# Neighbour sums on one core: output scaling moved to ScalarE, self terms added by the transfer, buckets decoded by shift and xor

## The chip, the core and the metric

The kernel runs on one core of a Trainium2 chip. A core has a matrix engine (PE; PEld is its weight load), a vector engine (DVE), an activation engine (ACT), a general engine (POOL) and a queue for transfers (SP); POOL and ACT issue transfers too, and 16 DMA engines carry all of them. Each engine runs its own instructions in order, and waits only on semaphores. The metric is the time on the device in microseconds (us), as the median of repeated executions; the profile is of one further execution.

## The reference

One layer of a graph network with mean aggregation: for 800,000 edges, the feature rows of the source nodes are summed at the destination nodes, scaled by `deg_inv`, and passed through a small weight.

```python
N, deg, D = 12500, 64, 64            # nodes, edges per node, features; E = N * deg

def reference(x, src, dst, deg_inv, w_self, w_neigh):
    nsum = _segment_sum(x[src], dst, N)          # (N, 64), random src and dst
    h_neigh = nsum * deg_inv[:, None]
    return x @ w_self + h_neigh @ w_neigh
```

## The kernel before

The edges are sorted first, and then gather and scatter both become matrix products with one-hot matrices.

**Keys and sort.** Each edge becomes a 32-bit key (`make_keys`): destination block of 144 nodes, source block of 128 nodes, then a bit for the half of the destination block and the two offsets inside the blocks. A pair of blocks is a bucket; there are 87 x 98 = 8526. 128 partitions sort 6250 keys each on DVE (`sort_runs`, L223 with copies on ACT at L225), the runs are cut at bucket borders, gathered by POOL (`gather_runs`, L461) and merged on DVE (`merge_runs`, L272 and L284 with copies on ACT at L268). The buckets are handled in two parts: part 0 has 41 buckets a row on 128 rows, part 1 has 27. The merge of part 1 is cut into steps that are dealt out by a written order (`after_sort`, `sums_and_merge`, under a manual schedule) between the decode of part 0 and the first tiles of the loop over buckets.

**Decode.** For each bucket POOL gathers a window of keys (`gather_window`, L621, tile `v`). `decode_buckets` works on four windows at once: `split` on DVE takes the bucket's base off the keys by xor (L668), counts on DVE the keys that belong there, with the count in `cnt` (L670), shifts the source offset out (L672, tile `w`) and masks the destination offset (L673); `narrow` on ACT turns both into 16-bit numbers (L678, L682) and stores the source offsets to `sl`; `turn` transposes the destination offsets on PE into `dlT`. Keys that lie beyond a window are found by `beyond`, and handled as extra edges ("leftovers"). The counts are summed at the end (`check`); if they don't come to the number of edges, a slow general path runs.

**Loop over buckets.** `one_hots` reloads `sl` for 28 buckets at a time to all partitions (tile `slb`, on SP's queue, L785) and compares it on DVE: `ohs` (L787) and `ohd` (L790). `nodes` goes over tiles of 8 buckets. PE picks source rows: `ct` <- `xh`, `ohs` (L815, three buffers in PSUM); ACT copies `ct` to `xg` (L825), and from tile 540 on DVE copies some of them (L823); PE sums at the destinations: `acc` <- `ohd`, `xg` (L871). Seven destination blocks make an octet, 86 tiles. At its end come the leftovers: their source rows are fetched by POOL (tile `lx`, L852, with an index that DVE copies out first, L850), and DVE makes their one-hots (tile `ohl`, L864, two instructions for each chunk of 128 keys).

**Output.** `self_terms` computes `x @ w_self` during the sort and stores it to a scratch tensor `own` in blocks of 1024 rows, through two buffers `os`. After an octet, `finish` handles its two blocks of 504 nodes, in steps dealt out between tiles: load `own` (tile `fo`, L923, SP's queue), multiply by `w_neigh` on PE (L939), copy the result to `o` on ACT (L940, one instruction of 256 columns), scale by `deg` on DVE (L945), add `fo` on DVE (L946), store to `out` (L947, POOL's queue; SP's for the last block).

## Time and profile before

| what | value |
|---|---|
| median of 3 runs | 2080.38 us (2077.32 to 2090.19) |
| the profiled execution | 2089.12 us, its span 2087.4 us |
| DVE busy | 1937.5 us, 93% of the span |
| ACT busy | 1257.6 us, 60% |
| PE busy | 1023.8 us, 49% |
| POOL busy | 589.7 us, 28% |
| moved | 330.78 MB, 158 GB/s over the span |

How to read it: a row of a group gives the line, the engine, the operation, output and input tiles with their shapes and the count, then the busy time in us and the mean duration of one in ns, and behind the second bar the idle time of the engine just before, with what ended it. A row of the waits names who waited, for whom, the total in us, how many times, and the longest. A row of the timeline begins with the start and the duration in us. The share of busy time is a mean over stages with different limits; what matters for a change is the stage in which it lies. The profiled execution lies 8.7 us above the median.

### The profile page before, as it was taken

The numbers are of one execution on the slowest core, as the hardware profiler recorded it, in microseconds if no ns is written. First come the engines' busy times: TensorE is split into PE (matmuls) and PEld (weight loads), VectorE is DVE, ScalarE is ACT, GpSimd is POOL, SyncE is SP. The second block draws the span as 40 slices with busy tenths as digits, with TensorE's granted clock in tenths as the row PEclk, the third lists the DMA queues.
The fourth block names the chain that finished last, engine by engine and source line by source line (L and its number), as shares of the span: only waits on it lengthen the run. The fifth ranks groups of instructions, "written<-read, shape, count | busy, mean of one in ns | idle before, by whom it ended". The sixth has DMA issues, their size and how long they took to land.

```text
span 2087.4 us, 59594 instructions
## 1 busy us (share of the span) xinstructions
PE 1023.8 (49%) x26057; PEld 887.0 (42%) x26057; DVE 1937.5 (93%) x2144; ACT 1257.6 (60%) x1779; POOL 589.7 (28%) x867
## 2 busy tenths in 40 slices
PE   0060000000000000000799999999987889989897
PEld 0050000000000000000688788788776778878786
DVE  8999999998999999999999899999999988988887
ACT  7470000078100010532799999999988788888886
POOL 1000000007898889878401010010152001000000
PEclk9999999999999999999999999999999999999999
DMA  4150000010100000111777787777876677777774
GB/s 152 48 115 9 0 0 0 16 47 17 23 20 22 13 14 11 53 54 50 273 292 286 261 285 280 273 277 268 306 268 251 222 288 286 291 268 284 269 286 161
DMA packets 108220, 330.78 MB, mean 158 GB/s; under 512 B 53680, under 2 KB 61824, under 8 KB 107440
## 3 DMA queue, kind: packets, MB, share of 16 engines
q1 hardware_dynamic: 90784, 306.65, 40.0%
q0 software_dynamic: 14352, 18.65, 4.2%
q8 instruction: 205, 3.36, 0.6%
q10 hardware_dynamic: 2816, 1.61, 0.3%
q14 instruction: 63, 0.52, 0.1%
HBM read 307.86 MB, written 18.99 MB: 157 GB/s over the span
## 4 chain that ended last, share of the span: by engine, by line
PE 37%; DVE 28%; POOL 19%; issue 10%; ACT 5%; DMA 1%; DVEq 0%; ACTq 0%; POOLq 0%; SPq 0%
PE ct L815 21%; PE acc L871 14%; POOL u L461 13%; DVE b L223 9%; DVE a L223 8%; POOL pad L372 3%; ACT xg L825 2%; POOL v L621 2%; DVE ohd L790 2%; DVE ohs L787 2%; DVE u L284 1%; PE po L939 1%; DVE xg L823 1%; DVE junkd L444 1%; ACT junk L598 1%
## 5 line engine op out<-in xcount | busy, mean ns | idle before, releaser
L825 ACT ACTIVATE xg<-ct 128x1024 f16<-128x1024 f32 (+1 forms) x991 | 935.2, 1111 | 104.0 <-PE ct L815 84.1
L815 PE MATMUL ct<-xh,ohs 128*128 128x128 f16 x8526 | 604.7, 222 | 52.5 <-issue 22.8
L815 PEld LDWEIGHTS <-ohs 128*128 128x128 f16 x8526 | 500.1, 99 | 98.4 <-issue 42.7
L284 DVE TENSOR_TENSOR u<-u 128x256 f32<-128x256 f32 (+47 forms) x494 | 452.2, 946 | 22.6 <-ACT u L268 15.6
L461 POOL DMA_INDIRECT u<-d,ix x256 | 327.3, 1279 | 470.6 <-DVE junkd L444 429.3
L871 PE MATMUL acc<-ohd,xg 64*128 64x72 f16 x17052 | 410.0, 195 | 52.9 <-issue 30.3
L787 DVE TENSOR_SCALAR ohs<-slb,pidx 128x3584 f16<-128x3584 bf16 x305 | 350.1, 1148 | 32.2 <-PE ct L815 30.4
L871 PEld LDWEIGHTS <-xg 64*128 64x128 f16 x17052 | 324.1, 95 | 128.6 <-issue 47.9
L790 DVE TENSOR_TENSOR ohd<-iota,dlT 128x2016 f16<-128x2016 bf16 x305 | 365.9, 1200 | 0.0
L688 PE MATMUL tr<-idb,l 128*128 128x128 bf16 x68 | 9.3, 277 | 463.9 <-ACT l L682 460.5
L268 ACT ACTIVATE u<-u 128x256 f32<-128x256 f32 (+15 forms) x94 | 47.4, 594 | 282.4 <-DVE u L272 282.4
L223 DVE TENSOR_TENSOR b<-a 128x3120 f32<-128x3120 f32 (+38 forms) x106 | 205.8, 1993 | 3.2 <-ACT junka L442 0.5
L688 PEld LDWEIGHTS <-l 128*128 128x128 bf16 x68 | 5.7, 120 | 467.1 <-ACT l L682 463.8
L223 DVE TENSOR_TENSOR a<-b 128x3114 f32<-128x3114 f32 (+33 forms) x92 | 189.2, 2104 | 3.1 <-ACT b L225 2.0
L947 POOL DMA_DIRECT2D out<-o x24 | 22.8, 952 | 574.5 <-DVE o L946 491.7
L451 PE MATMUL stp<-idf,st 128*128 128x128 f32 x2 | 0.9, 448 | 360.0 <-DVE st L449 360.0
L451 PEld LDWEIGHTS stp<-idf,st 128*128 128x128 f32 x2 | 0.4, 182 | 360.5 <-issue 360.5
L225 ACT ACTIVATE a<-b 128x1 f32<-128x1 f32 (+44 forms) x57 | 22.2, 423 | 204.0 <-DVE b L223 201.4
L823 DVE CAST xg<-ct 128x1024 f16<-128x1024 f32 x78 | 95.2, 1221 | 49.6 <-PE ct L815 49.5
L852 POOL DMA_INDIRECT lx<-xt,lxi x28 | 48.2, 1720 | 301.3 <-PE ct L815 165.8
L621 POOL DMA_INDIRECT v<-d,ix x68 | 90.8, 1335 | 61.0 <-ACT ix L651 43.6
L372 POOL MEMSET pad<- 128x89 f32 x457 | 90.3, 198 | 9.4
(135 smaller groups left out, 821.5 us busy)
## 6 DMA issues: line engine op xcount, KB each, us to landing
slb<-sl SPq DMA_DIRECT2D x305, 896.0 KB
u<-d,ix POOLq DMA_INDIRECT x256, 2.5
xt<-xh SPq DMA_DIRECT2D x1, 3136.0 KB
own<-os SPq DMA_DIRECT2D x12, 256.0 KB
fo<-own SPq DMA_DIRECT2D x24, 126.0 KB
out<-o POOLq DMA_DIRECT2D x24, 126.0 KB, 4.5
rd<-dst SPq DMA_DIRECT2D x4, 521.0 KB
rs<-src SPq DMA_DIRECT2D x4, 521.0 KB
```

Source lines behind the costliest of these rows:

```text
L223: nc.vector.tensor_tensor(view(dst, lo + sh, [[st, g], [1, l]]), x, y, op=op)
L284: nc.vector.tensor_tensor(to, at(cur, ln + lo, n), at(cur, lo + k, n), op=op)
L372: self.nc.gpsimd.memset(self.pad, 0.0)
L461: nc.gpsimd.indirect_dma_start(out=u[:nr, p * w:(p + 1) * w], out_offset=None, in_=src, in_offset=bass.IndirectOffsetOnAxis(ap=self.start[ ...
L621: self.nc.gpsimd.indirect_dma_start(out=self.v[:, k].bitcast(F32), out_offset=None, in_=flat(self.d2[part], 128 * PITCH2[part]), in_offset ...
L787: nc.vector.tensor_scalar(s.rearrange("p c s -> p (c s)"), b, self.pidx[:, :1], None, op0=OP.is_equal)
L790: nc.vector.tensor_tensor(d, self.iota[:, None].to_broadcast([128, 14, HN, 2]), ix, op=OP.is_equal)
L815: nc.tensor.matmul(ct[:, i * 128:(i + 1) * 128], cols[i][0], self.xh[:, (b0 + i) % NB].rearrange("p a f -> p (a f)"), start=True, stop=True)
L823: nc.vector.tensor_copy(xg[:, :cnt * 128], ct[:, :cnt * 128])
L825: nc.scalar.activation(xg[:, :cnt * 128], ct[:, :cnt * 128], AF.Copy)
L852: nc.gpsimd.indirect_dma_start(out=x, out_offset=None, in_=self.xt, in_offset=bass.IndirectOffsetOnAxis(ap=ix.bitcast(U32), axis=0))
L871: nc.tensor.matmul(acc[h][:, db % OCT * HN:(db % OCT + 1) * HN], xg[r, i * 128:(i + 1) * 128], d[r], start=db % OCT == 0 and sb == 0, stop ...
```

## The change

Four edits. **Output**: `finish` scales on ACT while it copies out of PSUM, with `deg` as a scale for each partition, one instruction for each of the four sets of 126 nodes (`add` is set in the loop over buckets); `self_terms` stores its rows to `out` as well as to `own`, and the block is then written by a transfer from POOL that adds to what stands in `out`. The load of `own`, its step, and both DVE operations go (the general path keeps the addition on DVE). **Decode**: shift and xor become one DVE instruction for each half of a window, against a base that is shifted beforehand; the count is taken from the shifted offsets, on ACT for part 0 and on DVE for part 1. **Leftovers**: the place of a key is numbered so that both halves of an octet lie side by side, and one DVE instruction makes both one-hots of a chunk. **Index**: the fetch of the source rows takes its index from where it stands.

```diff
@@ def setup(self):
-        self.c2 = [keep.tile([128, 5, KPRS[p]], F32, name=f"c2_{p}") for p in range(2)]
+        self.c2 = [keep.tile([128, 7, KPRS[p]], F32, name=f"c2_{p}") for p in range(2)]
...
-        self.wide = keep.tile([128, OCT * HN], FH, name="wide")
+        self.wide = keep.tile([128, 2 * OCT * HN], FH, name="wide")
...
@@ def self_terms(self, pool, mps):
-            nc.sync.dma_start(self.own[b0 * 128:(b0 + nb) * 128].rearrange("(b p) f -> p b f", p=128),
-                              o[:, :nb // 2].rearrange("p a b f -> p (a b) f"))
+            o = o.rearrange("p a b f -> p (a b) f")
+            nc.sync.dma_start(self.own[b0 * 128:(b0 + nb) * 128].rearrange("(b p) f -> p b f", p=128), o[:, :nb])
+            whole, rest = divmod(min(nb * 128, N - b0 * 128), 128)
+            r = b0 * 128 + whole * 128
+            nc.sync.dma_start(self.O["out"][b0 * 128:r].rearrange("(b p) f -> p b f", p=128), o[:, :whole])
...
@@ def decode_buckets(self, part, v, vp, mps):
         def split(k, n, vk, _):
-            vh = vk.rearrange("p k (h s) -> p k h s", h=2)
-            nc.vector.tensor_tensor(vh, vh, bases(k, n, H), op=OP.bitwise_xor)
             w = vp.tile([128, 4, 128], I32, name="w", bufs=2 + 2 * part)[:, :n]
-            nc.vector.tensor_scalar(w.bitcast(F32), vk, 1 << 14, None, op0=OP.is_lt, op1=OP.add,
-                                    accum_out=self.cnt[:, c0 + k // 4:c0 + k // 4 + 1])
-            nc.vector.tensor_scalar(w, vk, 7, None, op0=OP.logical_shift_right)
+            for h in range(2):
+                at = slice(h * H, (h + 1) * H)
+                base = view(self.c2[part].rearrange("p a k -> p (a k)").bitcast(I32), (5 + h) * kpr + k, [[1, n], [0, H]])
+                nc.vector.scalar_tensor_tensor(w[:, :, at], vk[:, :, at], 7, base,
+                                               op0=OP.logical_shift_right, op1=OP.bitwise_xor)
             nc.vector.tensor_scalar(vk, vk, 127, None, op0=OP.bitwise_and)
+            c = c0 + k // 4
+            if part:
+                nc.vector.tensor_scalar(self.junk(part)[:, :n * 128], w.rearrange("p k s -> p (k s)"), 128, None, op0=OP.is_lt, op1=OP.add,
+                                        accum_out=self.cnt[:, c:c + 1])
             return w

         def narrow(k, n, vk, w):
+            if part == 0:
+                c = c0 + k // 4
+                nc.scalar.activation(self.junk(part)[:, :n * 128], w.rearrange("p k s -> p (k s)"), AF.Sign, bias=self.edge[:, :1], accum_out=self.cnt[:, c:c + 1])
...
@@ def leftovers(self, part):
-        nc.vector.tensor_scalar(t, k, 1, 0x2000, op0=OP.logical_shift_right, op1=OP.bitwise_and)
+        nc.vector.tensor_scalar(t, t, float(OCTM), None, op0=OP.mult)
+        nc.vector.tensor_scalar(t, t, 8, 12, op0=OP.logical_shift_right, op1=OP.logical_shift_left)
         nc.vector.tensor_tensor(q, q, t, op=OP.add)
+        nc.vector.tensor_scalar(t, k, 14, 1, op0=OP.logical_shift_right, op1=OP.bitwise_and)
+        nc.vector.scalar_tensor_tensor(q, t, float(OCT * HN), q, op0=OP.mult, op1=OP.add)
...
@@ def nodes(self, pool, aps, mps):
-                ix = pool.tile([128, 1], I32, name="lxi", bufs=6)
-                nc.vector.tensor_copy(ix, self.left[p][1][:, c:c + 1])
+                ix = self.left[p][1][:, c:c + 1]
...
-                    for h in range(2):
-                        nc.vector.tensor_scalar(m[:, h, :width], self.wide[:, :width], place[:, c:c + 1],
-                                                -float(o * OCT * HN + h * 8192), op0=OP.subtract, op1=OP.is_equal)
+                    nc.vector.tensor_scalar(m.rearrange("p h n -> p (h n)"), self.wide, place[:, c:c + 1],
+                                            -float(o * (OCT * HN + 4096)), op0=OP.subtract, op1=OP.is_equal)
...
@@ def finish(self, qq, g, pool, mps, w, add=False):
-            nc.scalar.activation(o[:n, at], po[:n, at], AF.Copy)
+        for b0, nb, n, r in self.sets(qq):
+            for b in range(b0, b0 + nb):
+                nc.scalar.activation(o[:n, b], po[:n, b], AF.Copy, scale=self.deg[:n, 4 * qq + b:4 * qq + b + 1])
         yield
         for b0, nb, n, r in self.sets(qq):
             at = slice(b0, b0 + nb)
-            dg = self.deg[:n, 4 * qq + b0:4 * qq + b0 + nb, None].to_broadcast([n, nb, D])
-            nc.vector.tensor_tensor(o[:n, at], o[:n, at], dg, op=OP.mult)
-            nc.vector.tensor_tensor(o[:n, at], o[:n, at], own[:n, at], op=OP.add)
-            queue.dma_start(self.O["out"][r:r + nb * n].rearrange("(b p) f -> p b f", p=n), o[:n, b0:b0 + nb])
+            out = self.O["out"][r:r + nb * n].rearrange("(b p) f -> p b f", p=n)
+            if add:
+                nc.gpsimd.dma_start(out, o[:n, at], accum_op=OP.add)
...
```

Where instructions stand now, in the order of each engine. First ACT after the first octet, in the loop over buckets while the merge of part 1 runs (`g` is the sum of the octet, `xg` the picked rows of one tile). Before:

```order
L879 ACTIVATE g<-acc_2771 128x7x72
L879 ACTIVATE g<-acc_2772 128x7x72
L825 ACTIVATE xg<-ct 128x1024 x9
L940 ACTIVATE o<-po 126x256
L825 ACTIVATE xg<-ct 128x1024 x15
```

and now:

```order
L901 ACTIVATE g<-acc_2798 128x7x72
L901 ACTIVATE g<-acc_2799 128x7x72
L849 ACTIVATE xg<-ct 128x1024 x4
L959 ACTIVATE o<-po,deg 126x64 x4
L849 ACTIVATE xg<-ct 128x1024 x15
```

Four scaled copies stand where one copy stood, and five tiles earlier, since the step that loaded `own` is gone. Next DVE in the decode of part 0, one group of four windows and the merge steps that follow it. Before:

```order
L668 TENSOR_TENSOR v<-v,c_0_69 128x4x128
L670 TENSOR_SCALAR w,cnt<-v 128x512
L672 TENSOR_SCALAR w<-v 128x512
L673 TENSOR_SCALAR v<-v 128x4x128
L284 TENSOR_TENSOR u<-u 128x16x64
L284 TENSOR_TENSOR u<-u 128x16x68
```

and now:

```order
L685 SCALAR_TENSOR_TENSOR w<-v,c_0_69 128x4x64 x2
L687 TENSOR_SCALAR v<-v 128x4x128
L288 TENSOR_TENSOR u<-u 128x16x64
L288 TENSOR_TENSOR u<-u 128x16x68
L288 TENSOR_TENSOR u<-u 128x16x64
```

The two merge steps shown are the first of five, the three shown after the change are the first three of the same five. The xor, the count and the shift have become two instructions of half the size; the merge steps between the groups are the same ones in the same order.

More of the change, by code (lines that the diff above doesn't have):

```diff
@@ L64 @@
 OCT = 7
+OCTM = 256 // OCT + 1
+assert all((b * OCTM) >> 8 == b // OCT for b in range(NDB))
 def bid_base(b):
@@ L348, in setup @@
         nc.gpsimd.memset(self.cnt, 0.0)
+        self.edge = keep.tile([128, 1], F32, name="edge")
+        nc.gpsimd.memset(self.edge, -127.5)
         self.deg = keep.tile([FB, 4 * NQ], F32, name="deg")
@@ L585, in self_terms, with junk @@
             nc.scalar.activation(o[:, :nb // 2], po[:, :nb // 2], AF.Copy)
-            nc.sync.dma_start(self.own[b0 * 128:(b0 + nb) * 128].rearrange("(b p) f -> p b f", p=128),
-                              o[:, :nb // 2].rearrange("p a b f -> p (a b) f"))
+            o = o.rearrange("p a b f -> p (a b) f")
[3 more added lines that the diff above has]
+            nc.sync.dma_start(self.O["out"][b0 * 128:r].rearrange("(b p) f -> p b f", p=128), o[:, :whole])
+            if rest:
+                nc.sync.dma_start(self.O["out"][r:r + rest], o[:rest, whole])
+    def junk(self, part):
+        return self.keep.tile([128, max(n for _, n in WIN.w2[0] + WIN.w2[1])], BF, name=f"junk2{part}")
     def count_below(self, part, k, acc):
@@ L595, in count_below @@
         on = on_act2(part)
-        junk = self.keep.tile([128, max(n for _, n in WIN.w2[0] + WIN.w2[1])], BF, name=f"junk2{part}")
+        junk = self.junk(part)
         if on:
@@ L801, in nodes @@
         done = []
-        acc = ohl = lx = own = None
+        acc = ohl = lx = None
         turn = 0
@@ L885, in sums @@
                         late.append([b0 + 40 * (1 + 3 * q), self.finish(2 * o + q, g[:, q * 4 * FB:(q + 1) * 4 * FB],
-                                                                        self.fin, mps, self.w2n, own)])
+                                                                        self.fin, mps, self.w2n, True)])
             return last
@@ L903, in nodes @@
                     late[0][0] = b0 + 40
-            if t == len(tiles) - 12:
-                own = self.load_own(NQ - 1, self.fin)
             done.append(t)
@@ L954, in check @@
         nc.vector.memset(ones, 1.0)
+        nc.vector.tensor_scalar(self.cnt[:, :NCNT[0]], self.cnt[:, :NCNT[0]], -0.5, 256.0, op0=OP.mult, op1=OP.add)
+        rest = KPRS[0] % 4
+        if rest:
+            last = self.cnt[:, NCNT[0] - 1:NCNT[0]]
+            nc.vector.tensor_scalar(last, last, float(256 - 64 * rest), None, op0=OP.subtract)
         one = pool.tile([128, 1], F32, name="one")
```

20 lines of the change are left out of this document (11 added, 9 removed).

## The prediction

> **What bounds the kernel now.** First the busy time of each engine by stage; the columns are PE, weight loads, DVE, ACT and POOL (microseconds, instructions), the granted clock, the DMA share and GB/s.
>
> ```profile
> 0.00:894.00 894.00, 38.37 (x153) 32.05 (x153) 846.50 (x848) 261.82 (x630) 369.57 (x627) 1.00 0.12 33
> 894.00:1020.00 126.00, 21.32 (x365) 16.89 (x367) 120.50 (x202) 39.97 (x62) 109.59 (x154) 0.97 0.34 109
> 1020.00:1500.00 480.00, 452.92 (x11860) 390.14 (x11860) 456.10 (x478) 467.91 (x531) 35.28 (x22) 0.99 0.77 277
> 1500.00:1640.00 140.00, 111.89 (x2802) 96.78 (x2801) 135.12 (x214) 116.73 (x158) 45.65 (x39) 0.94 0.72 257
> 1640.00:2045.00 405.00, 368.38 (x10054) 324.12 (x10052) 351.24 (x373) 344.89 (x372) 25.20 (x23) 0.98 0.76 280
> ```
>
> DVE's 93% over the whole span hides five different limits. Stage 1 (to 894, the sort and the first merge) and stage 2 (to 1020, the decode of part 0 between merge steps) are DVE's: 95% and 96% busy while ACT and PE idle. In stage 3 (to 1500) ACT is fullest, 467.9 of 480; in stage 4 (to 1640, search and decode of part 1) DVE again, 135.1 of 140; in stage 5 nothing is full. So I looked at the waits of stages 3, 4 and 5, one row of each engine that matters:
>
> ```profile
> DVE ohs L787 <- PE ct L815: 21.3, 23, 2.5
> ...
> ACT xg L825 <- PE ct L815: 11.7, 17, 2.3
> ...
> PE acc L871 <- DVE xg L823: 7.0, 3, 3.4
> PE acc L871 <- DVE g L881: 5.8, 1, 5.8
> ...
> ACT xg L825 <- PE ct L815: 51.7, 97, 2.5
> ...
> DVE xg L823 <- PE ct L815: 43.4, 36, 3.2
> ...
> PE acc L871 <- issue: 14.5, 19, 1.8
> PE ct L815 <- issue: 11.3, 11, 1.9
> ```
>
> The first two rows are stage 3: DVE runs ahead and waits 21.3 us for PE to free one-hot buffers, ACT waits only 11.7. ACT's evictions of `ct` set the pace. The next two are stage 4: PE waits for DVE. The last four are stage 5: ACT and DVE both wait for PE, and PE mostly for "issue". A DVE saving therefore counts in stages 1, 2 and 4 alone, and ACT work that is added counts in stage 3.
>
> **Decode of part 0 (stage 2).** A full group of four windows costs DVE the first five rows here; the sixth is the nearest kind to the new shift-and-xor, the seventh the nearest size.
>
> ```profile
> L668 DVE TENSOR_TENSOR v<-v,c 128x512 int32<-128x512 int32 x10 | 6.8, 677 | 0.0
> L670 DVE TENSOR_SCALAR_CACHE_REDUCE w<-v 128x512 f32<-128x512 int32 x10 | 6.9, 686 | 0.7
> L670 DVE DVE_READ_ACCUMULATOR w<-v 128x1 f32 x11 | 0.9, 82 | 0.0
> L672 DVE TENSOR_SCALAR w<-v 128x512 int32<-128x512 int32 x10 | 4.9, 487 | 0.3
> L673 DVE TENSOR_SCALAR v<-v 128x512 int32<-128x512 int32 x10 | 4.6, 463 | 0.3
> L401 DVE SCALAR_TENSOR_TENSOR s<-s,g 128x1042 int32<-128x1042 int32 x4 | 5.0, 1246 | 0.4
> L945 DVE TENSOR_TENSOR o<-o,deg 126x256 f32<-126x256 f32 x24 | 10.0, 418 | 0.0
> L946 DVE TENSOR_TENSOR o<-o,fo 126x256 f32<-126x256 f32 x24 | 10.2, 425 | 0.8
> ```
>
> Before: 0.677 + 0.686 + 0.082 + 0.487 + 0.463 = 2.40 us. After: two shift-and-xors of 256 columns and the mask of 0.463. From 512 to 1042 columns a two-tensor operation grows by (1.246 - 0.677)/530 = 1.07 ns a column, so 256 columns cost 1.246 - 786 x 1.07 ns = 0.40; L945 says 0.418. I take 0.42: 1.30 us a group, 1.1 saved, ten groups 11.0, and half of one for the small eleventh: 11.5 us. Ends: 12.5 if 256 columns cost half of L668, 5.8 if each costs as much as all of L668.
>
> Two things may take some back. ACT now counts each group of part 0 (one instruction of 512 columns and an accumulator read) ahead of narrowing it; ACT is busy 40 of 126 us here, which hides it, except where a merge copy on ACT stands behind it and DVE waits for that copy. And DVE may catch up with the gathers. Group 7 starts in the first row below and needs the gather of the second:
>
> ```profile
> 960.65 0.69 DVE L668 TENSOR_TENSOR v<-v,c 128x512 int32<-128x512 int32 x1
> 948.22 1.02 POOL L621 DMA_INDIRECT v<-d,ix  x1 [0.16 <-issue]
> DMA to landing us min/median/max: 2.6/3.3/7.4
> ```
>
> The window lands at 948.2 + 3.3 = 951.5, 9.1 us ahead of its use. Seven groups save 7.7, so 1.4 remain: just enough. I take **-10** us, between -12.5 and -4.
>
> **Scaling on ACT (stage 3).** Each block of 504 nodes now takes four ACT instructions of 64 columns with a scale per partition, instead of one of 256. The new kind is not in the trace; its neighbours:
>
> ```profile
> 1098.31 0.80 ACT L940 ACTIVATE o<-po 126x256 f32<-126x256 f32 x1
> 1098.68 6.84 ACT L825 ACTIVATE xg<-ct 128x1024 f16<-128x1024 f32 x7
> ...
> 1184.92 0.70 ACT L940 ACTIVATE o<-po 126x256 f32<-126x256 f32 x1
> 1185.18 1.89 ACT L268 ACTIVATE u<-u 128x728 f32<-128x728 f32 x3
> ...
> L940 ACT ACTIVATE o<-po 126x256 f32<-126x256 f32 x10 | 5.9, 594 | 0.2 <-PE po L939 0.2
> L940 ACT ACTIVATE o<-po 126x256 f32<-126x256 f32 x9 | 3.6, 404 | 3.9 <-PE po L939 3.6
> L940 ACT ACTIVATE o<-po 26x64 f32<-26x64 f32 x1 | 0.2, 213 | 0.4 <-PE po L939 0.4
> L549 ACT ACTIVATE w2n<-wn,part 128x64 f32<-128x64 f32 x1 | 0.3, 346 | 0.0
> ```
>
> In stage 3's full queue the old instruction holds ACT from its start to the next one's: 0.37 us at 1098, 0.26 at 1185. Where ACT waits anyway (the nine of stage 5) it lasts 0.404, so neighbours overlap by 0.03 to 0.14; say 0.1. A 64-column instruction lasts 0.213 without a scale operand and 0.346 with one; in the queue that is 0.11 to 0.25 each, 0.45 to 1.0 for four, and 1.38 without overlap. I take 0.85, nearer to the row that has the operand, against 0.35: +0.5 for each of the ten in stage 3, **+5** us, between 0 and +10. Stage 3's row has no room that hides it.
>
> The Trainium skill, "ScalarE: Activation LUTs", What ACT_TABLE_LOAD costs, gives 186 ns + 0.833 ns a column, about 93 more for a per-partition operand, and about 93 of overlap; by it the four hold ACT 0.96 us, and the term is an estimated +6. Its Rules for kernel authors put a plain multiplication on VectorE, not ScalarE, which speaks against this move; the trace agrees for stage 3, where ACT and not DVE is full.
>
> DVE loses two operations a block there (0.418 + 0.425), the index copies, and half of the extra one-hot instructions:
>
> ```profile
> L864 DVE TENSOR_SCALAR ohl<-wide,lp 128x504 f16<-128x504 f16 x52 | 14.5, 344 | 0.0
> L864 DVE TENSOR_SCALAR ohl<-wide,lp 128x216 f16<-128x216 f16 x4 | 0.8, 268 | 0.0
> L850 DVE COPY lxi<-ls 128x1 int32<-128x1 int32 x28 | 4.0, 145 | 0.0
> ```
>
> 288 more columns cost 76 ns, so 1008 cost 0.344 + 0.133 = 0.48 where two cost 0.69: 0.21 saved a chunk; at L945's rate it would be a loss of 0.5. In stage 3 this is 10 x 0.84 + 12 x 0.15 + 10 x 0.21 = 12 us, behind 21.3 us that DVE already waits: 0, and -12 if I misread the bound.
>
> **Stage 4.** DVE: seven groups lose 2.40 and gain 1.30 + 0.77 (the count stays here), 0.33 each: 2.3. Three blocks 2.5, four chunks 0.8, two index copies 0.3, against three added small operations in the leftovers at L850's size, 0.4: 5.5. DVE sets this stage, so **-5**; -6.5 to -1, as PE or ACT may be late next.
>
> **Stage 5.** DVE loses another 12 us by the same sums and ACT gains 9 x 0.5 = 4.5, both smaller than the 43.4 and 51.7 us that they wait for PE: **0**, between -3 (PE sometimes waits for an eviction queued behind the removed pair) and +4.
>
> **The transfers.** In stage 1 every block of self terms is also stored to `out`, from the same two `os` buffers: 13 more transfers of 256 KB. In the loop 24 reads of `own` leave SP's queue, and 24 writes to `out` become read-add-write:
>
> ```profile
> 105.00:110.00 5.00, 4.12 (x18) 3.31 (x17) 5.00 (x3) 2.15 (x5) 0.00 (x0) 1.00 0.20 52
> 112.71 0.60 ACT L585 ACTIVATE os<-pw 128x512 f32<-128x512 f32 x1 [2.21 <-PE pw L583]
> out<-o POOLq DMA_DIRECT2D x24, 126.0 KB, 4.5
> 2073.20 0.84 POOL L947 DMA_DIRECT2D out<-o  x1 [12.93 <-DVE o L946]
> 2081.24 0.84 SPq L947 DMA_DIRECT2D out<-o  x2
> ```
>
> The first row holds one such store: 0.20 of 5 us, 1.0 us of all 16 engines. The `os` eviction waits 2.2 us for PE anyway, so a store that is 1.0 longer should not hold it: 0 for stage 1, at most +3 where the stores queue behind the large one of `xt` and a sort copy stands behind an eviction on ACT. A transfer of 126 KB takes 0.5 of the engines. No row shows an adding one; its bounds are the 0.5 less the read that is gone, and the whole 4.5 us to landing. Both lie below the room: nine blocks in 405 us at a share of 0.76 leave 0.24 x 45 = 10.8 us each. So 0 in the loop. At the end it counts: the last two transfers move from SP (0.84 us for both) to POOL (0.84 each) and land later by an unknown read, while four DVE operations ahead of them, at most 2 x 0.84 us, go. **+1.5**, between -1 and +5.
>
> **Sum.** -10 + 5 - 5 + 0 + 1.5 = -8.5 us. The profiled execution took 2089.1 us (span 2087.4), 8.7 above the median of 2080.4. It becomes 2080.6, and on the median's scale **2072**.
>
> **Rivals.**
> *Small gains, dear scaling.* The gathers on POOL slow the decode (-4), the scale operand does not overlap (+10), stage 4 gives -3, stage 5 +2, the end +3: +8, 2088. For it: the 1.4 us of room, and the lone 0.346. Against: ACT overlaps everywhere in stage 3.
> *DVE is the bound after all.* Then its relief counts in stages 3 and 5 too: -10 - 12 - 5 - 6 (half of stage 5's) + 1.5 = -31, 2049. For it: DVE is 95% busy in stage 3. Against: the 21.3 us of waiting for PE.
> *The adding transfer crowds the queue (slower).* Its pieces are 256 bytes and stand among the `slb` loads, which with the rest fill 0.76 of the engines, and among PE's instruction loads. If each of the 24 stops PE once for the longest "issue" seen, 1.8 us, that is +43: 2115. It decides from about 10.8 us of engine time per transfer, some twenty times the plain write's 0.5. For it: PE's stalls of 1.8 us exist already. Against: the plain transfer lands in 4.5.
> The Trainium skill, "DMA: Bandwidth & Descriptors", Rules for kernel authors, says that an adding DMA reads its destination and writes it later; taken as three movements it is an estimated 1.5 us, far from that point. No run here shows it.
>
> **Chances.** Forecast 0.50, small gains 0.16, DVE bound 0.14, crowding 0.20. A measurement of this kernel tells about 1%, 21 us. Faster by more: 0.16 (the DVE case and a little of the forecast); slower by more: 0.22 (crowding, and a little of the dear scaling); within: 0.62. The range goes from 2049, the DVE case, to 2098, ten above the small gains for the ends of stage 1 and of the last transfer; it leaves out the crowding.
>
> **What would show it.** Decode groups of 1.3 us on DVE, and the loop over buckets beginning some 10 us earlier. The four scalings 0.2 to 0.25 us apart, ACT still the fullest in stage 3, and that stage longer by about 1%. Waits of DVE for PE that grow in stages 3 and 5 by what DVE lost. Wrong would be: DVE waiting for the window gathers in stage 2, `ohs` waiting for `slb` by more than a few us, or PE's "issue" time well above its 26 us in stage 5.

## The result, and the profile after

The changed kernel takes 2082.99 us (median of 20 runs, 2073.43 to 2092.62), the kernel before 2081.61 (20 runs, 2071.49 to 2094.62): a ratio of 1.0005, with a 95% interval of 0.999 to 1.0021. Nothing was gained, where 8.5 us were forecast, though the time lies inside the stated range of 2049 to 2098. The profiled execution took 2089.37 us, its span 2087.3; that of before 2089.12, so the two traces can be laid side by side.

The stages of the changed kernel, with the columns of the table of before (stage 2 now ends at 1008):

```profile
0.00:894.00 894.00, 35.69 (x153) 29.71 (x153) 845.96 (x841) 261.76 (x630) 373.75 (x628) 0.57 0.14 36
894.00:1008.00 114.00, 20.39 (x354) 16.08 (x355) 108.52 (x181) 46.50 (x83) 102.81 (x135) 0.54 0.35 116
1020.00:1500.00 480.00, 454.04 (x11723) 389.21 (x11722) 442.96 (x431) 467.73 (x556) 45.92 (x34) 0.99 0.77 274
1500.00:1640.00 140.00, 116.54 (x2810) 99.28 (x2805) 129.50 (x197) 116.95 (x169) 46.73 (x40) 0.94 0.75 252
1640.00:2045.00 405.00, 368.55 (x9964) 323.42 (x9963) 339.15 (x330) 344.40 (x394) 34.47 (x23) 0.98 0.77 274
```

The granted clock of stages 1 and 2 is lower here than before (0.57 and 0.54 against 1.00 and 0.97), but PE has little work there, and of the 20 runs the 15 with the lower mean clock have a median of 2083.5 us, the other five 2082.5. DVE's work fell by 12 us in stage 2, 13 in stage 3, 6 in stage 4 and 12 in stage 5, close to what was worked out. The decode of part 0 became what was forecast. First its groups of instructions, then the first one-hot of the loop over buckets, of the changed kernel:

```profile
L685 DVE SCALAR_TENSOR_TENSOR w<-v,c 128x256 int32<-128x256 int32 x20 | 7.5, 417 | 1.0 <-DMA v<-d,ix 1.0
L697 ACT ACTIVATE junk<-w,edge 128x512 bf16<-128x512 int32 x10 | 7.2, 720 | 35.4 <-DVE w L685 30.0 <-issue 5.4
L687 DVE TENSOR_SCALAR v<-v 128x512 int32<-128x512 int32 x10 | 4.3, 430 | 0.3
...
986.86 1.15 DVE L811 TENSOR_SCALAR ohs<-slb,pidx 128x3584 f16<-128x3584 bf16 x1 [0.30 <-ACT u L272]
```

and the same one-hot before:

```profile
998.41 1.15 DVE L787 TENSOR_SCALAR ohs<-slb,pidx 128x3584 f16<-128x3584 bf16 x1 [0.61 <-DMA slb<-sl]
```

The loop starts 11.5 us earlier, and DVE waits only 1.0 us for window gathers. So those 11.5 us are lost again inside the loop and behind it. The end of an octet can be read on ACT, which then copies `acc` to `g`. The copies that end octets 1, 5, 8 and 12, and the short last one, of before:

```profile
1089.22 1.36 ACT L879 ACTIVATE g<-acc 128x504 f32<-128x504 f32 x2
1428.75 1.24 ACT L879 ACTIVATE g<-acc 128x504 f32<-128x504 f32 x2
1707.73 0.59 ACT L879 ACTIVATE g<-acc 128x504 f32<-128x504 f32 x1 [0.23 <-PE acc L876]
2040.86 0.59 ACT L879 ACTIVATE g<-acc 128x504 f32<-128x504 f32 x1 [0.23 <-PE acc L876]
2078.60 0.35 ACT L879 ACTIVATE g<-acc 128x216 f32<-128x216 f32 x1 [0.85 <-PE acc L876]
```

and after, with the tail behind them:

```profile
1081.08 1.18 ACT L901 ACTIVATE g<-acc 128x504 f32<-128x504 f32 x2
1420.32 1.23 ACT L901 ACTIVATE g<-acc 128x504 f32<-128x504 f32 x2
1705.85 0.59 ACT L901 ACTIVATE g<-acc 128x504 f32<-128x504 f32 x1 [0.23 <-PE acc L898]
2038.96 0.59 ACT L901 ACTIVATE g<-acc 128x504 f32<-128x504 f32 x1 [0.22 <-PE acc L898]
2075.31 0.35 ACT L901 ACTIVATE g<-acc 128x216 f32<-128x216 f32 x1 [0.85 <-PE acc L898]
2077.04 0.90 ACT L959 ACTIVATE o<-po,deg 126x64 f32<-126x64 f32 x4 [1.38 <-PE po L956]
2078.06 2.29 POOL L965 DMA_DIRECT2D out<-o  x2 [15.04 <-ACT o L959]
```

The lead is 8.1 us after octet 1, 8.4 after octet 5, 1.9 after octet 8 and 3.3 after the last. So in this pair of profiles octets 2 to 5, which lie in stage 3, took as long as before (339.2 us against 339.5), and so did octets 9 to 12 (333.1 both times); the lead went in octets 6 to 8 (285.5 us against 279.0), before octet 1 ended, and in the tail. Behind the last octet the tail to the span's end grew from 8.8 us (2078.6 to 2087.4) to 12.0 (2075.3 to 2087.3): POOL takes 2.29 us to issue the two last transfers, SP took 0.84.

One profile of each doesn't show where the middle part goes. An octet shifts by several us from one execution to the next (octet 9 took 83.1 and 89.1 us in the two profiles of the kernel with the decode edit alone, below), and single runs of one kernel spread over 20 us. So the experiments go by medians, each against the kernel before on the same chip.

### The profile page after: what moved, and what is told of

It is laid out like the page before. It is cut to its first block, busy times and chain, and to the rows that moved or that the text cites. A ratio compares the mean times of both kernels' runs of the same rounds, so it can differ in the third digit from the quotient of the medians.

```text
span 2087.3 us, 59522 instructions
## 1 busy us (share of the span) xinstructions
PE 1035.3 (50%) x26057; PEld 892.1 (43%) x26057; DVE 1902.8 (91%) x2022; ACT 1273.6 (61%) x1875; POOL 621.6 (30%) x870
## 4 chain that ended last, share of the span: by engine, by line
DVE 35%; PE 32%; issue 12%; POOL 10%; ACT 8%; DMA 1%; DVEq 0%; ACTq 0%; POOLq 0%; SPq 0%
PE ct L839 19%; PE acc L893 12%; DVE b L227 9%; DVE a L227 9%; POOL u L467 7%; DVE u L288 7%; ACT xg L849 5%; DVE u L320 2%; POOL v L635 2%; POOL pad L378 2%; DVE u L276 1%; DVE ohs L811 1%; DVE ohd L814 1%; PE po L956 1%; DVE junkd L450 1%
## 5 line engine op out<-in xcount | busy, mean ns | idle before, releaser
L839 PE MATMUL ct<-xh,ohs 128*128 128x128 f16 x8526 | 611.7, 222 | 48.6 <-issue 18.9
L467 POOL DMA_INDIRECT u<-d,ix x256 | 341.2, 1333 | 469.6 <-DVE junkd L450 428.3
L893 PE MATMUL acc<-ohd,xg 64*128 64x72 f16 x17052 | 416.3, 195 | 48.5 <-issue 28.5
L965 POOL DMA_DIRECT2D out<-o x26 | 45.5, 1772 | 803.7 <-ACT o L959 611.5
L276 DVE TENSOR_TENSOR u<-u 128x512 f32<-128x512 f32 (+21 forms) x68 | 75.7, 1145 | 7.7 <-issue 3.9
```

The source lines that it names most:

```text
L276: nc.vector.tensor_tensor(at(oth, to, n), x, y, op=op)
L467: nc.gpsimd.indirect_dma_start(out=u[:nr, p * w:(p + 1) * w], out_offset=None, in_=src, in_offset=bass.IndirectOffsetOnAxis(ap=self.start[ ...
L839: nc.tensor.matmul(ct[:, i * 128:(i + 1) * 128], cols[i][0], self.xh[:, (b0 + i) % NB].rearrange("p a f -> p (a f)"), start=True, stop=True)
L893: nc.tensor.matmul(acc[h][:, db % OCT * HN:(db % OCT + 1) * HN], xg[r, i * 128:(i + 1) * 128], d[r], start=db % OCT == 0 and sb == 0, stop ...
```

## Experiments

**Which edit costs.** Decode edit alone:

```diff
@@ kernel before, split()
-            nc.vector.tensor_tensor(vh, vh, bases(k, n, H), op=OP.bitwise_xor)
...
+                nc.vector.scalar_tensor_tensor(w[:, :, at], vk[:, :, at], 7, base, ...)
```

> The kernel before with the decode edit alone (shift and xor in one operation, count on ACT for part 0). Theory A, the output edit eats the decode's gain: the loop over buckets starts 11 to 12 us earlier as in the changed kernel, PE's pace carries this to the end, and the time falls by about 11 us (ratio 0.995). Rival B, the gain is lost between the loop's start and its end whatever the output does, since a later stage is set by something that doesn't start earlier: the loop starts 11 to 12 us earlier, and the time stays within 3 us of the kernel before. Rival C, the second part's decode has become dearer in the trace than thought: the octets gain 8 to 12 us until 1430 us and lose 5 or more between 1500 and 1700 us.

Measured: 0.9948 [0.9921, 0.9974] (the ratio to the kernel before, and its 95% interval), 10.9 us less. Output edit alone:

```diff
@@ kernel before, finish() and self_terms()
+                nc.scalar.activation(o[:n, b], po[:n, b], AF.Copy, scale=self.deg[:n, 4 * qq + b:4 * qq + b + 1])
...
+                nc.gpsimd.dma_start(out, o[:n, at], accum_op=OP.add)
```

> The kernel before with the output edit alone (scaling on ACT, self terms stored to the result early, blocks added by the transfer). Theory A: slower by about 10 us (ratio 1.005), made up of 4 to 5 us in stage 3 (ACT), 3 us at the end (the last adding transfer), and 2 to 3 us between. Rival B: within 3 us of the kernel before, since the loop's end is set by something that neither edit moves. My forecast's own terms for this edit: +5 in stage 3, -2.5 in stage 4, 0 in stage 5, +1.5 at the end, together +4.

Measured: 1.0075 [1.0046, 1.0103], 15.7 us more. Theory A holds: the decode's gain stays to the end when nothing else is changed, and the output edit eats it. The theory had added up about 10 us for it, the lower end of its interval (9.6 to 21.5). The third and fourth edits without the output edit (the changed kernel, `finish`, `self_terms` and the load of `own` as before):

```diff
@@ changed kernel, finish()
-                nc.gpsimd.dma_start(out, o[:n, at], accum_op=OP.add)
+            nc.vector.tensor_tensor(o[:n, at], o[:n, at], dg, op=OP.mult)
+            nc.vector.tensor_tensor(o[:n, at], o[:n, at], own[:n, at], op=OP.add)
```

> The changed kernel without the output edit: decode, leftovers and index edits alone. By theory A (the output edit eats the decode's gain) it keeps what decode_alone gave, about 11 us (ratio 0.995). If the leftovers and index edits pay of their own by relieving DVE, it lies 2 to 4 us lower still (0.993); if their longer one-hots (1008 columns at once) hold DVE at the octets' ends, it lies higher, at 0.997 to 1.0.

Measured: 0.997 [0.9948, 0.9993]. It can't be told from the decode edit alone; the leftovers and index edits are worth nothing that shows.

**Which part of the output edit.** Five kernels take one part out, or put one part in.

```diff
@@ changed kernel: scaling left out
-                nc.scalar.activation(o[:n, b], po[:n, b], AF.Copy, scale=self.deg[:n, 4 * qq + b:4 * qq + b + 1])
+            nc.scalar.activation(o[:n, at], po[:n, at], AF.Copy)
```

> The changed kernel with the scaling by the degrees left out: one copy of 256 columns on ACT in place of four scaled ones. If the scaling on ACT costs what it holds ACT for in stage 3 (0.45 us more for a block, ten blocks) and that is all, the time falls by 4 to 5 us against the changed kernel (ratio to the kernel before 0.998). If the four instructions cost beyond that, because each eviction of ct behind them holds up PE too in stages 4 and 5, it falls by 8 to 10 us (0.996). If the scaling costs nothing, it stays at 1.0005.

```diff
@@ changed kernel: adding left out
-                nc.gpsimd.dma_start(out, o[:n, at], accum_op=OP.add)
+                nc.gpsimd.dma_start(out, o[:n, at])
```

> The changed kernel with the blocks stored plainly by POOL in place of added: the self terms are left out of the result. If the adding transfer costs only at the end, the tail after the last octet falls from 12 to 9 us and the time by 3 us against the changed kernel (ratio to the kernel before 0.999). If the adding transfers slow the loop too (their packets stand in the queues with the slb loads), it falls by 6 us or more (below 0.998), with less issue time on PE in stage 5. If neither, no change (1.0005).

```diff
@@ changed kernel: the place of the product by the small weight
+        if add:
+            yield
```

> The changed kernel with an empty step in place of the one that loaded the self terms, so that PE multiplies by the small weight five tiles later, where it did before. If the output edit costs its 10 us or more because that product now follows the octet's copies too closely (PE waiting for g, or its PSUM buffer taken from ct at a bad place), this gives most of it back: 8 us or more below the changed kernel (ratio to the kernel before 0.9965). If the place doesn't matter, 1.0005 as for the changed kernel.

```diff
@@ without the output edit: early stores alone
+            nc.sync.dma_start(self.O["out"][b0 * 128:r].rearrange("(b p) f -> p b f", p=128), o[:, :whole])
```

> The kernel without the output edit, with the early stores of the self terms to the result added (13 more transfers in the sort; the result is written over later). If these stores cost what I put them at, 0 to 3 us, the ratio lies at 0.995 to 0.9965. If they are the missing cost of the output edit, by holding the self terms' buffers and so sort copies on ACT, it lies at 1.0 or above and the loop starts some 10 us later than without them.

```diff
@@ without the output edit: scaling on ACT alone
-            nc.scalar.activation(o[:n, at], po[:n, at], AF.Copy)
+                nc.scalar.activation(o[:n, b], po[:n, b], AF.Copy, scale=self.deg[:n, 4 * qq + b:4 * qq + b + 1])
...
-            nc.vector.tensor_tensor(o[:n, at], o[:n, at], dg, op=OP.mult)
```

> The kernel without the output edit, with the scaling alone moved from DVE to ACT: four scaled copies in the place of one copy, DVE adds the self terms as before. My forecast's term is +5 us in stage 3 and 0 elsewhere, less 1.2 in stage 4: ratio 0.997 against 0.995 without it. If scaling is free, as leaving it out of the changed kernel suggested, 0.995. If the scaling itself is the missing cost, 1.0.

| kernel | ratio to the kernel before | 95% interval |
|---|---|---|
| scaling left out | 1.0006 | 0.9984 to 1.0029 |
| adding left out | 1.0003 | 0.9981 to 1.0026 |
| product five tiles later | 1.0002 | 0.9981 to 1.0024 |
| without output edit, early stores | 0.9958 | 0.9936 to 0.998 |
| without output edit, scaling on ACT | 0.9994 | 0.9971 to 1.0018 |

The early stores and the place of the product cost nothing that shows, so two suspects fall. The scaling put in costs 5 us (0.997 to 0.9994, with intervals that overlap), yet leaving it out gives nothing back, and neither does leaving out the adding. Each interval is about 5 us wide to a side: a part of up to some 5 us can hide in it. So the next kernels make each part larger.

**Each part made larger.** ACT: the four scalings four times over, and twice (with 2 in the place of the 4).

```diff
@@ changed kernel, finish()
-            for b in range(b0, b0 + nb):
+            for b in [*range(b0, b0 + nb)] * (4 if add else 1):
                 nc.scalar.activation(o[:n, b], po[:n, b], AF.Copy, scale=...)
```

> The changed kernel with the scaling of each block done four times over on ACT: sixteen instructions in place of four, which hold ACT for about 0.8 us for each four, so 2.4 us more a block. By my forecast (ACT is the bound of stage 3) ten blocks there give +24 us and the rest little: ratio to the kernel before 1.012 to 1.016 (1.0005 plus 24 to 33 us). By the rival that the evictions have slack and the scaling costs nothing, it stays within 5 us of the changed kernel: below 1.003.

> The changed kernel with the scaling done twice over on ACT: eight instructions a block, 0.8 us more than four. Three more sets of four cost 54.6 us, with PE waiting 41 us for the last scaled copy to free its PSUM buffer, a wait that the changed kernel doesn't show. If the cost is linear, one more set costs 18 us (ratio 1.009), and the one that the change added costs about half of that. If it is a threshold, since two other buffers cover the first microsecond or two, one more costs under 8 us (below 1.004), and the change's own scaling about nothing.

Measured: 1.0267 [1.0237, 1.0297] and 1.007 [1.0048, 1.0093]: three more sets cost 54.6 us, one more 13.5. Neither a threshold nor free; the second set's cost is known to about 6 us to either side. In the changed kernel's queue one set holds ACT from 1085.68 to 1086.49, 0.81 us:

```profile
1085.68 1.03 ACT L959 ACTIVATE o<-po,deg 126x64 f32<-126x64 f32 x4
1086.49 2.06 ACT L849 ACTIVATE xg<-ct 128x1024 f16<-128x1024 f32 x2
```

25 blocks make 20 us for a set, of which 13.5 (two thirds) reach the end for the second, and 18 each on average of three. The octets say where; the same copies as above with the scaling four times over:

```profile
1079.95 1.13 ACT L901 ACTIVATE g<-acc 128x504 f32<-128x504 f32 x2
1441.06 1.42 ACT L901 ACTIVATE g<-acc 128x504 f32<-128x504 f32 x2
1741.71 0.59 ACT L901 ACTIVATE g<-acc 128x504 f32<-128x504 f32 x1 [0.23 <-PE acc L898]
2098.02 0.59 ACT L901 ACTIVATE g<-acc 128x504 f32<-128x504 f32 x1 [0.23 <-PE acc L898]
```

Octets 2 to 5 take 361.1 us against 339.2, octets 6 to 8 300.7 against 285.5, octets 9 to 12 356.3 against 333.1: +22, +15 and +23 (this profile is of the slowest of seven runs, 14 us above their median). ACT's added time counts in stage 5 as it does in stage 3, although ACT there waits for PE for 56.5 us in the changed kernel, and still for 46.4 from octet 9 on with the scaling four times over. The way it does so is a wait that the changed kernel doesn't have. The waits of PE from 1020 to the end, scaling twice:

```profile
PE ct L839 <- ACT o L959: 7.5, 18, 0.8
```

and four times:

```profile
PE ct L839 <- ACT o L959: 40.9, 22, 2.4
```

`po` takes one of the three PSUM buffers of `ct` until ACT has made its last copy. Of the 40.9 us, 21.7 fall before 1500 and 15.4 behind octet 8. To this comes PE's clock: with the scaling four times over, the granted clock is 0.96 in 1020 to 1500 and 0.94 in 1640 to 2045, where the changed kernel has 0.99 and 0.98. That is another 14 and 16 us of PE at full speed.

The transfers: three more adding ones, or three more plain ones, for each of 23 blocks, to rows of the scratch tensor (the plain ones without the last argument).

```diff
@@ changed kernel, finish()
                 nc.gpsimd.dma_start(out, o[:n, at], accum_op=OP.add)
+                for k in (6, 12, 18) if qq < NQ - 2 and n == FB else ():
+                    s = (qq + k) % (NQ - 1) * 4 * FB
+                    nc.gpsimd.dma_start(self.own[s:s + nb * n].rearrange("(b p) f -> p b f", p=n), o[:n, at],
+                                        accum_op=OP.add)
```

> The changed kernel with four adding transfers for each block but the last two: three more add the same block to rows of the scratch tensor that nothing reads any more. POOL issues 69 more of 1.6 us and the DMA engines carry 69 more transfers of 126 KB; POOL's other work in the loop (window gathers of part 1, fetches of extra source rows) stands behind them. If the adding transfers crowd the queues and stop PE, as in my third rival, three more of them cost at least three times what the one costs: with 0.3 us for each, 20 us (1.010). If they are free in the loop, below 1.003, except where a window gather of part 1 behind them is late, at most 5 us.

> As the kernel with four adding transfers, but the three more are plain writes of the same rows to the same places; the first one still adds. The three more adding ones cost 24.6 us for 69, 0.36 us each. If it is the adding that costs (twice the packets, a read and a write), the three plain ones cost at most a third of that: 8 us, ratio to the kernel before below 1.005. If any transfer from POOL costs the same, 1.011 to 1.013; then the adding one in place of a plain one is free, and only the loads of the self terms that are gone could have paid for it.

Measured: 1.0123 [1.0087, 1.0159] and 1.0071 [1.0043, 1.0099]. 69 more adding transfers cost 24.6 us, 0.36 each; 69 more plain ones 13.7, 0.20 each. Transfers from POOL aren't free in the loop, plain ones neither. That an adding one is dearer is less sure: the difference of 10.9 us is hardly more than its own uncertainty, some 9.5 us. The third rival's way would show as PE's "issue" time. From 1020 to 2045, the changed kernel:

```profile
PE acc L893 <- issue: 28.5, 32, 2.7
PE ct L839 <- issue: 16.5, 23, 3.0
```

with four adding transfers a block:

```profile
PE acc L893 <- issue: 42.5, 38, 2.8
PE ct L839 <- issue: 27.6, 23, 3.5
```

and with one adding and three plain ones:

```profile
PE acc L893 <- issue: 42.5, 41, 2.3
PE ct L839 <- issue: 23.5, 24, 2.6
```

and the kernel before:

```profile
PE acc L871 <- issue: 29.7, 35, 1.8
PE ct L815 <- issue: 21.3, 21, 2.7
```

45.0, 70.1, 66.0 and 51.0 us. The rises of 25 and 21 us look like the costs of 24.6 and 13.7, but they don't show the way. The same two rows add up to 68.3 us in the kernel without the output edit, which has no transfer more than the kernel before, and to 62.8 with the scaling left out; and the change itself didn't raise them. What the added transfers take of the DMA engines can be read. POOL's queue on the pages of the two kernels (packets, MB, share of 16 engines over the span), adding and plain:

```profile
q0 software_dynamic: 68368, 27.71, 10.8%
q0 software_dynamic: 31936, 27.69, 7.3%
```

Against the changed kernel's 5.7%, 69 adding transfers take 109 us of all 16 engines, 1.6 each, and 69 plain ones 34 us, 0.5 each. So an adding one holds the engines about three times as long as a plain one. Whether its price comes from there or from PE's instruction loads isn't shown.

DVE: the dropped pair three times over, on a tile that nothing reads.

```diff
@@ changed kernel, finish()
+                for _ in range(3):
+                    nc.vector.tensor_tensor(idle[:n, at], o[:n, at], dg, op=OP.mult)
+                    nc.vector.tensor_tensor(idle[:n, at], idle[:n, at], o[:n, at], op=OP.add)
```

> The changed kernel with three times the pair of DVE operations that it dropped, on a tile that nothing reads: 2.5 us more of DVE work a block, 62 us in all. By my forecast DVE has room in stages 3 and 5 (it waits 35 and 59 us for PE there) and none in stage 4: 3 x 2.5 = 7.5 us there and little elsewhere, ratio 1.003 to 1.006. If DVE is the bound after all, 35 us or more in stages 3 and 4: 1.018 and above. If the relief of DVE itself made the loop slower, the ratio falls below 1.0.

Measured: 1.0078 [1.0052, 1.0104], 15 us for 62 us of DVE work. The end of octets 6 and 8 with it:

```profile
1508.72 0.59 ACT L901 ACTIVATE g<-acc 128x504 f32<-128x504 f32 x1 [0.23 <-PE acc L898]
1718.16 0.59 ACT L901 ACTIVATE g<-acc 128x504 f32<-128x504 f32 x1 [0.23 <-PE acc L898]
```

The changed kernel ended octet 6 at 1508.90 and octet 8 at 1705.85: +12.5 us between the two, where four blocks put 12 pairs on DVE, 10.2 us. At the end of octet 6 it was not behind (it had ended octet 1 3.3 us earlier). In the other kernels with one set of scalings or none, octets 7 and 8 took some 189 to 203 us, here 209.4. DVE has room in stage 3 and little or none in stage 4, as the forecast had it.

The tail: the last block as before.

```diff
@@ changed kernel, finish()
+            if own is not None and add:
+                nc.vector.tensor_tensor(o[:n, at], o[:n, at], own[:n, at], op=OP.add)
+                nc.sync.dma_start(out, o[:n, at])
```

> The changed kernel with the last block written as before: its self terms loaded ahead, added on DVE, stored from SP's queue. The tail behind the last octet falls from 12 us to about 9, and the time by 3 us: ratio to the kernel before 0.999 against 1.0005. If the tail is not what it costs, no change.

Measured: 1.0015 [0.999, 1.0039]. In its profile the tail falls from 12.0 to 8.3 us; the median doesn't show those 3.7 us.

**Both parts together, and a version that beats both kernels.**

```diff
@@ changed kernel: scaling and adding left out
+            nc.scalar.activation(o[:n, at], po[:n, at], AF.Copy)
...
+                nc.gpsimd.dma_start(out, o[:n, at])
```

> The changed kernel with both left out: the scaling (one copy of 256 columns) and the adding (plain store by POOL, so the self terms are missing too). If the two cost 8 to 10 us together and each alone was lost in the spread of the runs, the ratio is 0.996 to 0.9975. If neither costs anything and the output edit's loss lies elsewhere, it stays at 1.0005 as with either one.

Measured: 0.9933 [0.9908, 0.9958]; with the decode edit alone, in the same hour on the same chip:

```diff
@@ kernel before, split(): the decode edit, once more
+                nc.vector.scalar_tensor_tensor(w[:, :, at], vk[:, :, at], 7, base, ...)
```

> The kernel before with the decode edit alone, once more, on the chip and in the hour of the other three. It measured 0.9948 [0.9921, 0.9974]; with the leftovers and index edits added it was 0.997 [0.9948, 0.9993]. If those two are neutral, both are about 0.996 and this lies there again; if they cost a few us, this stays at 0.995. Either way it should beat both kernels by 5 us or more (below 0.9975).

it was 0.9943 [0.9917, 0.9969]. Leaving out both gives 15 us back, about all that the output edit cost.

```diff
@@ changed kernel: scaling back on DVE, adding kept
+            nc.scalar.activation(o[:n, at], po[:n, at], AF.Copy)
...
+            nc.vector.tensor_tensor(o[:n, at], o[:n, at], dg, op=OP.mult)
```

> The changed kernel with the scaling back on DVE (one copy on ACT, one multiplication on DVE) and the block still added by the transfer. If the scaling on ACT costs about 6 to 8 us of the output edit's loss, as the mean of the runs so far says, the ratio is 0.9965 to 0.9985. If it costs nothing, as leaving the scaling out of the changed kernel suggested (1.0006), 1.000 to 1.0015, with DVE's 0.42 us a block paid in stage 4 only. If it carries nearly all of the loss, 0.995.

Measured: 0.9967 [0.9944, 0.9991], 8 us below the changed kernel in a kernel that computes everything. Yet the kernel with the scaling left out, which does less, had 1.0006 [0.9984, 1.0029]: the two intervals hardly overlap, so the 8 us are not a firm size. The step the other way takes ACT's copy out altogether:

```diff
@@ decode edit alone, finish()
-            nc.scalar.activation(o[:n, at], po[:n, at], AF.Copy)
+            nc.vector.tensor_tensor(o[:n, at], po[:n, at], dg, op=OP.mult)
         yield
...
-            nc.vector.tensor_tensor(o[:n, at], o[:n, at], dg, op=OP.mult)
```

> The kernel before with the decode edit, and the copy on ACT of each block dropped: DVE multiplies by the degrees straight out of PSUM, at the step where ACT copied. ACT loses 0.3 to 0.4 us a block, DVE nothing to speak of. If ACT time counts in the loop at the 0.5 to 0.7 that the repeated scalings gave, 4 to 6 us less than the decode edit alone: 0.992 against 0.9945. If the PSUM buffer of po is held longer, since DVE has one-hots and merge steps of several us ahead of it, PE waits for that buffer (a new wait of ct for DVE's o) by up to 1 us a block, and the ratio rises to 0.997 or above.

Measured: 0.9917 [0.9888, 0.9946], 2072.96 us beside 2090.72 for the kernel before on the same chip. It is the fastest version here, some 6 us below the decode edit alone (six runs, and the intervals overlap). DVE reads PSUM at the price of SBUF, 0.423 us where the old multiplication took 0.418, and the feared wait is small:

```profile
L955 DVE TENSOR_TENSOR o<-po,deg 126x256 f32<-126x256 f32 x24 | 10.2, 423 | 21.1 <-PE po L953 21.0
...
DVE o L955 <- PE po L953: 22.4, 17, 2.9
...
PE ct L829 <- DVE o L955: 0.3, 1, 0.3
```

DVE now waits 22.4 us for PE, in time that it has; PE waits 0.3 for DVE.

## Why the prediction was right and wrong

The prediction failed on the output edit. Its terms for that edit were +5 for the scaling in stage 3, -2.5 for the blocks' DVE work in stage 4, 0 for stage 5 and for the transfers in the loop, and +1.5 for the tail: +4. Alone, the edit measured +15.7 (9.6 to 21.5). As far as the runs show, the two zeros are the step that failed: ACT work that is added in stage 5 counts, and a transfer from POOL has a price in the loop. The decode's gain came as forecast, so the two cancelled, and that the time landed inside the range is no merit of the sum.

- **Decode of part 0, -10: right.** -11.5 at the loop's start, and -10.9 and -11.9 (0.9943 of 2084) at the end where it stands alone. The two shift-and-xors took 0.417 us each against 0.42.
- **Scaling on ACT, +5 in stage 3: the place is what failed.** The hold of 0.81 us was sized rightly (0.85). Wrong was that "ACT work that is added counts in stage 3" and nowhere else, and with it the zero for stage 5, where 4.5 us of ACT were set against 51.7 us that ACT waits for PE. That wait is no room: ACT's copies and PE's matmuls take turns on three PSUM buffers, and with the scaling two and four times over PE waits 7.5 and 40.9 us for the last scaled copy, in stage 5 too, even if ACT idles 15% of that stage. For the first set this is argued: in the changed kernel no such wait shows, and its profile doesn't show the longer stage 3 that the forecast gave as a sign (octets 2 to 5 as long as before). Put back on DVE, the scaling gave 8 us (about 6 to either side), left out nothing; the second set cost 13.5. The Trainium skill, "ScalarE: Activation LUTs", Rules for kernel authors, puts a plain multiplication on VectorE; the pair of kernels that computes everything agrees (1.0005 with it on ACT, 0.9967 on DVE).
- **Transfers in the loop, 0: wrong.** I set a transfer's share of the DMA engines against their idle share, and got room. An adding one took 1.6 us of the engines (the estimate ahead of the runs was 1.5), well inside the 10.8 us of room, and the added ones still cost 0.36 us each, plain ones 0.20. That is the third rival's sign at a fifth of the 1.8 us it assumed; its way, stops of PE, isn't shown, and the sign that was named for it, "issue" well above 26 us in stage 5, didn't come (25.7). The change replaced 24 plain ones by 24 adding ones, 24 x 0.16 = 4 us, from a difference that is itself hardly clear of noise; what the loads of `own` that went were worth isn't shown.
- **Tail, +1.5: mis-sized.** +3.2 in the profile, inside its range; POOL's issue took 2.29 us against SP's 0.84, and from its end to the span's end went about 7 us against 5.3.
- **Stage 4, -5: DVE's bound was right, the gain isn't to be seen.** DVE work that is added there costs about all that it takes (12.5 us for 10.2, one profile each). In the profile octets 6 to 8 took 285.5 us against 279.0; with the decode edit alone 276.1 and 277.6 in its two profiles. PE's long stall there, 4.8 us behind DVE's copy of `g`, stayed.
- **DVE relief in stages 3 and 5, 0: right.** DVE's wait for PE in stage 3 grew from 21.3 to 34.8 us, by what DVE lost.

The sum by what was measured: -11 + 8 + 4 + 3 = +4, against 1.4 (-2 to +4.4). How the output edit's 15 us split stays open: scaling left out gave nothing, adding left out gave nothing, both together 15. Two costs that simply add don't fit: both left out would then give 1.0006 + 1.0003 - 1.0005 = 1.0004, and 0.9933 was measured, further off than the intervals allow. Ten kernels here have the decode, leftovers and index edits and nothing multiplied; put in groups, they say it roughly. With neither part the mean ratio is 0.9954 (0.997, 0.9958, 0.9933), with the adding alone 0.9987 (1.0006, 0.9967), with the scaling alone 0.9999 (1.0003, 0.9994), with both 1.0007 (1.0005, 1.0002, 1.0015). So by these means one part alone costs 7 or 9 us, and the other on top of it only 2 or 4: they overlap in part. Kernels of one group lie up to 8 us apart, so this is a direction and not a size. Which waits carry the first set of scalings stays open too; PE's wait for `o` first shows with the second.

## What to carry to other kernels

An engine that waits a lot for another may have no room if the two take turns on a few buffers: before moving work to it, look at who holds the buffers while the new work runs, and multiply it in a trial kernel, since an effect under the spread of the runs is hard to see otherwise. Don't put a transfer at nothing because the DMA engines have idle time; here even plain ones had a price (0.20 us each). A wait that is longer in a slower kernel may be called the cause only if it is short in the fast ones too; PE's "issue" time here was not. And when several edits land together, time each one alone: here one edit kept 11 us that another hid.

## What the runs showed of the hardware

PE paid for a stall twice. The timeline of PE in the changed kernel, around its longest stall in stage 4:

```profile
1613.23 1.12 PE L893 MATMUL acc<-ohd,xg 64*128 64x72 f16 x31 [4.80 <-DVE g L903]
1614.28 1.89 PE L839 MATMUL ct<-xh,ohs 128*128 128x128 f16 x16
1616.10 1.14 PE L893 MATMUL acc<-ohd,xg 64*128 64x72 f16 x32
...
1623.81 1.07 PE L839 MATMUL ct<-xh,ohs 128*128 128x128 f16 x16
```

and its granted clock there, the third number from the right:

```profile
1612.00:1612.50 0.50, 0.00 (x0) 0.00 (x0) 0.50 (x2) 0.00 (x0) 0.00 (x0) 0.83 0.00 0
1612.50:1613.00 0.50, 0.00 (x0) 0.00 (x0) 0.50 (x2) 0.00 (x0) 0.00 (x0) 0.50 0.00 0
...
1622.50:1623.00 0.50, 0.50 (x11) 0.50 (x10) 0.00 (x0) 0.11 (x1) 0.00 (x0) 0.93 0.95 72
```

After a stall of 4.8 us the clock is at half for 10.2 us (about 1612.33 to 1622.57, by the partial slices), and sixteen matmuls take 1.89 us where they take 1.07 at the full clock. 10.2 is three times 3.41. The Trainium skill, "TensorE: Matmul & The Clock Gate", Part 1: The HAM clock gate, gives a free-running window of 3413 ns and the full clock after at least one busy window; the length agrees, and here two whole windows with PE at work passed first, since PE had work from 1613.2 on and was slow until 1622.6. So this stall cost about twice its length: 4.8 us of waiting, and half of the 9.3 us that PE then worked at half clock. That fits that DVE work in stage 4 costs a little more than itself. From 1020 to 2040 the changed kernel has eleven half-clock times, nine of 3.4 us, one of 6.8 and this one, which take some 24 us of PE at full speed; the kernel before has nine, which take some 20.

An adding transfer is dearer for POOL as well as for the DMA engines. The groups of the transfers, before:

```profile
L947 POOL DMA_DIRECT2D out<-o x24 | 22.8, 952 | 574.5 <-DVE o L946 491.7 <-DVE ohs L787 82.8
```

and after:

```profile
L965 POOL DMA_DIRECT2D out<-o x26 | 45.5, 1772 | 803.7 <-ACT o L959 611.5 <-ACT xg L849 192.1
```

0.95 us became 1.77. POOL's queue (the page's part on queues: packets, MB, share of 16 engines) before:

```profile
q0 software_dynamic: 14352, 18.65, 4.2%
```

and after:

```profile
q0 software_dynamic: 27520, 18.76, 5.7%
```

Almost twice the packets carry the same bytes.
